# New prices in the build-time planner of a transformer layer, and pair sums in twos for two head groups of each unit

## The chip, the cores and the metric

One core of a Trainium2 chip runs the whole kernel. The metric is the device time in microseconds (us). The engines are TensorE (PE; its weight loads are a row of their own, PEld), VectorE (DVE), ScalarE (ACT), GpSimd (POOL) and SyncE (SP), whose queue issues the DMAs. Each engine works through its own list of instructions strictly in order; semaphores hold an instruction until what it needs is done.

## What is computed

A pre-norm transformer layer on 2048 tokens of width 1024, with 32 heads of 32, and an FFN of width 3584, in bf16:

```
h  = x + softmax(q k^T / sqrt(32)) v @ wo,   q, k, v = layernorm(x) @ wqkv
h2 = h + gelu(layernorm(h) @ w1 + b1) @ w2 + b2       # gelu in its tanh form
```

## The kernel before

**Units, jobs, rounds.** The tokens are cut into 8 units of 256 queries, the heads into 8 groups of 4. A job is one unit with one group (64 jobs), a round is 256 keys of a job (8 rounds). In a round PE makes the scores of four heads as 8 small matmuls in row tiles (`qk`, L787), ScalarE takes the exp in two instructions of 128 x 1024 (L797, 1024 in all), and PE multiplies by V in column tiles (`pv`, L840). Scores go through three pairs of PSUM banks; a new `qk` needs two pairs.

**Denominators.** VectorE adds the two key blocks of a round into a tile PS (L855, "pair sum"), and PE multiplies PS by a matrix of ones, 4 matmuls (`den`, L878). Where `QUAD(qb, g)` is true, VectorE also adds the pair sums of two rounds (L861), and one `den` step serves both. The last round of a job goes to PE without any sum, and so do all rounds of the first two jobs. `QUAD` is `qb < QA or g < QG`, with QA = 2 and QG = 0: true for units 0 and 1. `finish` transposes the denominators (L895), copies the numerators (L902), inverts (L906), transposes back (L907) and multiplies (L909).

**The rest ("background").** Layer norm: `bn_stats` twice and `bn_aggr` on VectorE, a power on POOL, a `tensor_scalar`; then transposes on PE and their eviction (L613, L620 on ScalarE, L622 on VectorE). Projections go through `mm`, with full tiles (L541, L544) or as four narrow ones (L538). For every unit follow wo (eviction L949), a layer norm, ffn1 (14 blocks, eviction with the bias into gT on VectorE, L1018), gelu and ffn2 (output L1070). All of this uses two PSUM banks, 6 and 7, shared with the jobs' accumulators. Gelu works on 1024 columns: x*x (L1038), an affine step (L1039), times x (L1040), all on VectorE, each reading the one before; tanh on ScalarE (L1041, 49 times); plus one (L1042) and times x (L1043) on VectorE. The last unit's gelu is one instruction on ScalarE.

**The order.** Nothing is ordered by hand. `Graph.schedule` plays the whole program through at build time: each task has a price `occ` (how long it holds its engine) and a latency `lat` (how long after that a reader can start), and whenever an engine is free it takes a ready task by priority and then by number. Pair sums have priority -2, the reads of `finish` and the evacuations by ScalarE and the tanh -1, evictions 0, gelu's VectorE steps 1; on PE `qk` goes first, `pv` and `den` come in batches, background fills. SP's DMAs are tasks of the same play. The resulting lists are what the engines get. Prices set the order alone: `assign` puts semaphore waits on all dependences; for engines other than PE this includes a dependence on an earlier instruction of the same engine:

```
elif d.eng != t.eng or t.eng != E.PE:      # kept as a wait
```

`release` sets when a task counts as ready. It leaves out the latency for a dependence within PE, whose instructions follow one another without a wait.

Of the kernel before, what the change touches and what calls it, by code (L numbers as in the profile page):

```python
# [8 lines left out]
ALU = mybir.AluOpType  # L9
AX = mybir.AxisListType  # L10
E = mybir.EngineType

P = 128
# [47 lines left out]
class Graph:  # L61
# [47 lines left out]
    def schedule(self, pick_pe, pool, switch=0.1, dma_rate=280.0, dma_lat=2.1, dma_issue=0.06):  # L109
# [11 lines left out]
        n = 0  # L121
        num = {t: i for i, t in enumerate(self.tasks)}

        def release(t):
            t.ready = max([d.done - (d.lat if d.eng == t.eng == E.PE else 0.0) for d in t.deps], default=0.0)
            heapq.heappush(upcoming[t.eng], (t.ready, num[t], t))
            heapq.heappush(events, t.ready)

# [5 lines left out]
        def free_banks(now):  # L134
            out = []
            for b, u in pool.items():
                if isinstance(u, list) and all(x.done is not None and x.done <= now + 1e-9 for x in u):
                    out.append(b)
            return out

        while n < total:
# [5 lines left out]
            for e in self.ENGS:  # L147
                while free[e] <= now + 1e-9:
# [31 lines left out]
                    if e == E.SP:  # L180
                        k = min(range(self.n_lanes), key=lambda i: lanes[i].done if lanes[i] else 0.0)
# [147 lines left out]
def build_kernel(nc, A_x, A_wqkv, A_wo, B_w1, B_b1, B_w2, B_b2, out):  # L329
    _, S, D = A_x.shape  # L330
# [9 lines left out]
    EPS_BF = 1.0013580322265625e-05  # L340
# [11 lines left out]
    gr = Graph(N_LANES)  # L352
# [65 lines left out]
    rr, B_rr = sb(top, "rr", [P, 2, 8], F32, 2)  # L418
# [51 lines left out]
    psum = nc.alloc_psum_tensor("ps", [P, 8, 512], F32)  # L470
# [11 lines left out]

    MM = 0.2195
    def c_dve_ps(n):
        return (120 + n) / 960.0 + 0.02

    def c_dve(n, x=1):
        return (62 + n / x) / 960.0 + 0.02

    def c_tt(n):  # L490
        return n / 1920.0 + 0.155

    def c_ts(n):
        return n / 3840.0 + 0.165

    GELU_PRIO = 1

    def c_act(n, ap_bias=False):
        return 0.073 + (0.093 if ap_bias else 0.0) + n / 1200.0

    def pe(fns, occ, reads=(), writes=(), kind="bg", mode="full", prio=0, after=()):
        return gr.add(E.PE, fns, occ, 0.16, reads, writes, prio, kind, mode, after)
# [13 lines left out]
    def bi(bank):  # L516
        return bank.n if isinstance(bank, Slot) else bank

    def bb(bank):
        return bank.buf if isinstance(bank, Slot) else B_ps[bank]  # L520
# [26 lines left out]
        return t  # L547

    def act(fn, n, reads=(), writes=(), prio=0, ap_bias=False, kind="", after=()):
        return gr.add(E.Activation, fn, c_act(n, ap_bias), 0.14, reads, writes, prio, kind, after=after)  # L550

    def dve(fn, occ, reads=(), writes=(), prio=0):
        return gr.add(E.DVE, fn, occ, 0.08, reads, writes, prio)

    def pool(fn, occ, reads=(), writes=(), prio=0):
        return gr.add(E.Pool, fn, occ, 0.1, reads, writes, prio)

    def dma(out_ap, in_ap, nbytes, reads=(), writes=(), prio=0, noncontig=False, after=()):
        def fn(s):
# [10 lines left out]
         reads=[B_ident], writes=[B_ident])  # L570
# [8 lines left out]
    def layer_norm(tiles, prio, norm="dve", quick=False):  # L579

        n = len(tiles)
        while cnt["ln"] % NLN + n > NLN:
            cnt["ln"] += 1
        i = cnt["ln"] % NLN
        cnt["ln"] += n
        for k, (x_ap, B_x, o_ap, B_o) in enumerate(tiles):
            for c in range(2):
                dve(lambda v, c=c, k=k, x_ap=x_ap: v.bn_stats(st_l[:, i + k, 6 * c:6 * c + 6], x_ap[:, 512 * c:512 * c + 512]),  # L588
                    0.68, reads=B_x if isinstance(B_x, list) else [B_x], writes=[B_stl[i + k]], prio=prio)
            dve(lambda v, k=k: v.bn_aggr(mv_l[:, i + k, :], st_l[:, i + k, :]), 0.2,  # L590
                reads=[B_stl[i + k]], writes=[B_mv[i + k]], prio=prio)
        sl = slice(i, i + n)
        if quick:
            dve(lambda v: v.tensor_copy(mvb[:, sl, :], mv_l[:, sl, :]), 0.17, reads=B_mv[sl], writes=B_mvb[sl], prio=prio)
            dve(lambda v: v.tensor_scalar(tb[:, sl, :], mvb[:, sl, 1:2], EPS_BF, None, ALU.add), 0.17,
                reads=B_mvb[sl], writes=B_tb[sl], prio=prio)
        else:
            pool(lambda g: g.tensor_copy(mvb[:, sl, :], mv_l[:, sl, :]), 0.25, reads=B_mv[sl], writes=B_mvb[sl], prio=prio)
            pool(lambda g: g.tensor_scalar(tb[:, sl, :], mvb[:, sl, 1:2], EPS_BF, None, ALU.add), 0.25,
                 reads=B_mvb[sl], writes=B_tb[sl], prio=prio)  # L600
        dve(lambda v: v.tensor_copy(mvr[:, sl, :], mvb[:, sl, 0:1]), 0.17, reads=B_mvb[sl], writes=B_mvr[sl], prio=prio)
        pool(lambda g: g.tensor_tensor(denb[:, sl, 0], tb[:, sl, 0], cexp[:, 0:n], ALU.pow), 0.42 + 0.157 * n,
             reads=B_tb[sl] + [B_cexp], writes=B_denb[sl], prio=prio)
        dve(lambda v: v.reciprocal(rden[:, sl, 0], denb[:, sl, 0]), 0.19, reads=B_denb[sl], writes=B_rden[sl], prio=prio)
        for k, (x_ap, B_x, o_ap, B_o) in enumerate(tiles):
            eng, cost = (dve, 0.58) if norm == "dve" else (pool, 3.8)
            eng(lambda e, k=k, x_ap=x_ap, o_ap=o_ap: e.tensor_scalar(
                o_ap, x_ap, mvr[:, i + k, :], rden[:, i + k, :], ALU.subtract, ALU.mult), cost,
                reads=(B_x if isinstance(B_x, list) else [B_x]) + [B_mvr[i + k], B_rden[i + k]], writes=[B_o], prio=prio)

    def transposes(src_ap, B_src, bank, dst_ap, B_dst, evac, prio):
        for dc in range(DC):
            t = pe(lambda p, dc=dc: p.transpose(psb[:, bi(bank), dc * P:(dc + 1) * P], src_ap[:, dc * P:(dc + 1) * P], ident[:]),  # L613
                   0.064, reads=[B_src, B_ident], writes=[bb(bank)], prio=prio)
            take(t, bank)

        def src():
            return psb[:, bi(bank), :].rearrange("p (dc t) -> p dc t", dc=DC)
        if evac == "act":
            t = act(lambda a: a.activation(dst_ap, src(), ACT.Copy), 1024, reads=[bb(bank)], writes=[B_dst], prio=-1)  # L620
        else:
            t = dve(lambda v: v.tensor_copy(dst_ap, src()), 0.70, reads=[bb(bank)], writes=[B_dst])  # L622
        drop(t, bank)


# [178 lines left out]

    closing = set()
    QA = 2
    QG = 0
    DA = 0

    def QUAD(qb, g):  # L810
        return qb < QA or g < QG

# [3 lines left out]
    class Job:  # L816
# [69 lines left out]
        def finish(self):  # L886
            qb, g, bank, nq = self.qb, self.g, self.bank, self.nq
            u = qb % 3
            o = cnt["od"] % 2
            cnt["od"] += 1  # L890
            B_O, B_D = B_OD[o]
            final = self.final
            od, dd = OD[:, o, 0, 0:nq], OD[:, o, 1, 0:nq]
            D = dd.rearrange("p (b j) -> p b j", j=32)
            t = dve(lambda v: v.transpose(dd, psum[:, bi(bank), nq:2 * nq]), c_dve_ps(nq),  # L895
                    reads=[self.B_O, self.B_D], writes=B_D, prio=-1)
            drop(t, bank)
            if final:
                t = act(lambda a: a.activation(od, psum[:, bi(bank), 0:nq], ACT.Copy), nq,
                        reads=[self.B_O, self.B_D], writes=B_O, prio=-1, after=[t])  # L900
            else:
                t = dve(lambda v: v.tensor_copy(od, psum[:, bi(bank), 0:nq]), c_dve_ps(nq),  # L902
                        reads=[self.B_O, self.B_D], writes=B_O, prio=-1)
            drop(t, bank)
            nb = nq // 32
            dve(lambda v: v.reciprocal(rr[:, o, 0:nb], D[:, :, 0]), 0.15, reads=B_D, writes=[B_rr[o]], prio=0)  # L906
            dve(lambda v: v.transpose(D, rr[:, o, 0:nb].unsqueeze(2).to_broadcast([P, nb, 32])), c_dve(nq),  # L907
                reads=[B_rr[o]], writes=B_D, prio=0)
            dve(lambda v: v.tensor_tensor(OT[:, u, g, 0:nq], od, dd, ALU.mult), c_dve(nq),  # L909
                reads=B_O + B_D, writes=B_OT[u][g][0:nq // P], prio=1)  # L910
# [437 lines left out]
```

## Time and profile before

| | |
|---|---|
| runs | 1092.40, 1092.58, 1096.39 us; median 1092.58 |
| profiled execution | 1093.21 us, span 1091.4 us |
| PE busy | 1047.8 us (96%) |
| ScalarE busy | 1019.5 us (93%) |
| VectorE busy | 789.4 us (72%) |
| POOL busy | 28.2 us (3%) |
| DMA | 175.44 MB, mean 161 GB/s |
| exp L797 | 1024 of 128 x 1024, mean 1168 ns, 954.0 us busy |
| pair sum L855 | 432, mean 687 ns, 288.5 us busy |
| sum of two pair sums L861 | 42, mean 687 ns, 28.9 us busy |
| den L878 from PS | 1560 matmuls of 128 x 32 by 256 |

The duration of an instruction is not the time from its start to the next one's: on VectorE and ScalarE instructions overlap in part, on PE they are pipelined and their ends are modelled, so a busy PE is not a PE at its peak. The first exp starts at 16.2 us and the last at 1027.3 us.

### The profile page before, as it was taken

To read this page: it belongs to the slowest core of one execution; us is meant where nothing else is said; L and a number is where in the kernel's file an instruction comes from. 1 tells how busy PE (TensorE), PEld (TensorE's weight loads), DVE (VectorE), ACT (ScalarE), POOL (GpSimd) and SP (SyncE) were. 2 spreads that over 40 slices of the span, in tenths; PEclk is the share of its full clock that TensorE was granted. 3 is DMA by queue.
4 is the path that set the end of the run, shared out by engine and by line. 5 is a ranking of instruction groups with operands and counts; after the bars stand their busy time and mean duration, and the time that the engine had idled before them with its cause. 6 is when DMAs were issued, how large, how long until landed. Compare 5 with 4: busy or idle time off the path is not lost.

```text
span 1091.4 us, 41529 instructions
## 1 busy us (share of the span) xinstructions
PE 1047.8 (96%) x18880; PEld 610.0 (56%) x18930; DVE 789.4 (72%) x1518; ACT 1019.5 (93%) x1124; POOL 28.2 (3%) x78
## 2 busy tenths in 40 slices
PE   7999999998999999999999999999999999999998
PEld 5655555553457446644565466447545754664483
DVE  7657777777778958886589669857885877786511
ACT  4889999999999999999999999999999999999750
POOL 2100000000000000000000000000000000000000
PEclk9999999999899999999999999999999999999999
DMA  7920120035366547555665486467566655975740
GB/s 190 250 83 2 41 83 5 2 133 181 118 186 181 165 154 238 166 174 183 219 176 158 151 249 183 139 193 224 147 199 201 182 173 153 330 225 178 236 156 20
DMA packets 266224, 175.44 MB, mean 161 GB/s; under 512 B 26944, under 2 KB 260416, under 8 KB 265664
## 3 DMA queue, kind: packets, MB, share of 16 engines
q1 hardware_dynamic: 266048, 172.79, 52.0%
q8 instruction: 148, 2.42, 0.9%
q14 instruction: 28, 0.23, 0.1%
HBM read 162.27 MB, written 10.49 MB: 158 GB/s over the span
## 4 chain that ended last, share of the span: by engine, by line
ACT 75%; PE 23%; DVE 1%; issue 1%; DMA 0%; SPq 0%
ACT PT L797 71%; PE ps L541 6%; PE ps L544 5%; PE ps L538 5%; ACT tg L1041 3%; PE ps L787 3%; PE ps L840 2%; PE ps L878 1%; ACT xnT L620 1%; DMA xrb<-in_A_x_dram 0%; PE ps L613 0%; SPq L563 0%; DVE gT L1018 0%; DVE xnT L622 0%; DVE st L588 0%
## 5 line engine op out<-in xcount | busy, mean ns | idle before, releaser
L797 ACT ACTIVATE PT<-ps 128x1024 bf16<-128x1024 f32 x1024 | 954.0, 1168 | 15.9 <-PE ps L787 15.8
L855 DVE TENSOR_TENSOR PS<-PT 128x1024 bf16<-128x1024 bf16 x432 | 288.5, 687 | 121.5 <-ACT PT L797 60.4
L787 PE MATMUL ps<-QT,KT 32*128 32x256 bf16 x4096 | 204.2, 273 | 11.6 <-ACT PT L797 8.1
L840 PE MATMUL ps<-PT,V 128*32 128x256 bf16 x4096 | 176.9, 273 | 2.1 <-ACT PT L797 1.3
L787 PEld LDWEIGHTS ps<-QT,KT 32*128 32x128 bf16 x4096 | 60.9, 92 | 174.0 <-ACT PT L797 162.4
L840 PEld LDWEIGHTS ps<-PT,V 128*32 128x32 bf16 x4096 | 105.0, 97 | 30.8 <-issue 8.3
L541 PE MATMUL ps<-hnT,a_w1r 128*128 128x256 bf16 x906 | 111.5, 273 | 0.7 <-DVE rr L906 0.3
L541 PE MATMUL ps<-a_w2r,gT 128*128 128x512 bf16 x430 | 106.6, 380 | 4.4 <-issue 1.6
L878 PE MATMUL ps<-PS,ones 128*32 128x256 bf16 x1560 | 109.7, 274 | 1.1 <-DVE PS L855 0.5
L538 PE MATMUL ps<-hnT,a_w1r 128*32 128x256 bf16 x2648 | 96.2, 274 | 7.3 <-DVE gT L1018 2.4
L541 PEld LDWEIGHTS ps<-hnT,a_w1r 128*128 128x128 bf16 x906 | 82.8, 98 | 24.8 <-issue 14.5
L538 PE MATMUL ps<-a_w2r,gT 128*32 128x512 bf16 x1304 | 96.5, 381 | 0.1
L1018 DVE TENSOR_TENSOR gT<-ps,b1f 128x512 bf16<-128x512 f32 x98 | 67.3, 687 | 25.5 <-PE ps L538 15.7
L538 PEld LDWEIGHTS ps<-hnT,a_w1r 128*32 128x32 bf16 x2648 | 65.3, 96 | 24.2 <-issue 18.1
L541 PEld LDWEIGHTS ps<-a_w2r,gT 128*128 128x128 bf16 x458 | 39.7, 98 | 52.6 <-issue 12.6
L1041 ACT ACTIVATE tg<-tg 128x1024 bf16<-128x1024 bf16 x49 | 57.9, 1185 | 0.0
L541 PE MATMUL ps<-xnT,Wall 128*128 128x512 bf16 (+1 forms) x238 | 52.2, 354 | 3.4 <-issue 1.3
L878 PEld LDWEIGHTS ps<-PS,ones 128*32 128x32 bf16 x1560 | 41.9, 96 | 17.5 <-issue 5.7
L541 PE MATMUL ps<-a_w1r,OT 128*128 128x512 bf16 x191 | 49.4, 393 | 0.0
L538 PEld LDWEIGHTS ps<-a_w2r,gT 128*32 128x32 bf16 x1304 | 29.2, 96 | 23.1 <-issue 15.0
L895 DVE STREAM_TRANSPOSE OD<-ps 128x256 f32<-128x256 f32 x64 | 28.6, 446 | 12.8 <-PE ps L878 6.5
L1070 DVE SCALAR_TENSOR_TENSOR b_ost<-ps,hch 128x512 bf16<-128x512 f32 x4 | 2.8, 692 | 45.3 <-PE ps L544 45.3
(92 smaller groups left out, 995.1 us busy)
## 6 DMA issues: line engine op xcount, KB each, us to landing
a_w2r<-in_B_w_dram SPq DMA_DIRECT2D x105, 512.0 KB, 5.5
a_w1r<-in_B_w_dram SPq DMA_DIRECT2D x98, 512.0 KB, 4.4
a_w1r<-in_A_wo_dram SPq DMA_DIRECT2D x32, 512.0 KB, 4.2
b_w1r<-in_B_w_dram SPq DMA_DIRECT2D x14, 512.0 KB, 5.3
a_w1r<-in_A_wqkv_dram SPq DMA_DIRECT2D x11, 512.0 KB, 4.5
xrb<-in_A_x_dram SPq DMA_DIRECT2D x16, 256.0 KB, 4.3
Wall<-in_A_wqkv_dram SPq DMA_DIRECT2D x16, 256.0 KB, 4.3
a_w2r<-x_scratch SPq DMA_DIRECT2D x8, 512.0 KB, 4.5
```

The lines of the kernel that those rows point to most:

```text
L538: fns.append(lambda p, j=j: p.matmul(psum[32 * j:32 * j + 32, bi(bank), c0:c1], lhsT[:, 32 * j:32 * j + 32], rhs, start=start, stop=stop, ...
L541: t.whole = lambda p: p.matmul(psum[:, bi(bank), c0:c1], lhsT, rhs, start=start, stop=stop, skip_group_check=True)
L544: t = pe(lambda p: p.matmul(psum[:, bi(bank), c0:c1], lhsT, rhs, start=start, stop=stop), occ, reads=reads, writes=[bb(bank)], mode="full" ...
L620: t = act(lambda a: a.activation(dst_ap, src(), ACT.Copy), 1024, reads=[bb(bank)], writes=[B_dst], prio=-1)
L787: return p.matmul(psum[:, 2 * us[h // 2] + h % 2, n * i:n * i + n], KT[32 * h:32 * h + 32, g, k0:k0 + P], QT[32 * h:32 * h + 32, qs, 0:n], ...
L797: act(lambda a, u=u, k=k: a.activation(PT[:, s, k, :, :], psum[:, 2 * u:2 * u + 2, :], ACT.Exp, bias=0.0, scale=SCALE), 1024, reads=[B_ps[ ...
L840: fns.append(lambda p, i=i, h=h: p.matmul(psum[32 * h:32 * h + 32, bi(bank), 0:nq], V[:, g, nk * r + i, 32 * h:32 * h + 32], PT[:, s, h // ...
L855: dve(lambda v: v.tensor_tensor(PS[:, n, :, :], pairs[:, :, 0:256], pairs[:, :, 256:512], ALU.add), c_dve(1024, 2), reads=[B_PT[2 * s], B_ ...
L878: fns.append(lambda p, h=h, rhs=rhs, i=i: p.matmul(psum[32 * h:32 * h + 32, bi(bank), nq:2 * nq], ones32[:, :], rhs, start=False, stop=las ...
L895: t = dve(lambda v: v.transpose(dd, psum[:, bi(bank), nq:2 * nq]), c_dve_ps(nq), reads=[self.B_O, self.B_D], writes=B_D, prio=-1)
L1018: drop(dve(lambda v: v.tensor_tensor(gT[:, fc:fc + 2, cs], psum[:, bi(bank), 0:2 * n].rearrange("p (f c) -> p f c", f=2), b1f[:, fc:fc + 2 ...
L1041: act(lambda a: a.activation(t, t, ACT.Tanh, bias=0.0, scale=math.sqrt(2.0 / math.pi)), c, reads=B_t, writes=B_t, prio=-1)
```

## The change

Three things, in one diff.

1. **Prices.** On VectorE and ScalarE, `occ` was close to an instruction's duration; it becomes the interval from one start to the next. An addition of 1024 columns goes from 0.688 to 0.600 us in gelu (and from 0.618 to 0.600 as a pair sum), an affine step of 1024 from 0.432 to 0.332, an eviction of 512 fp32 columns from 0.678 to 0.600, a `bn_stats` from 0.68 to 0.60, an exp or tanh of 1024 from 0.926 to 0.915. Latencies grow: ScalarE from 0.14 to 0.165, VectorE from 0.08 to 0.135.
2. **The release rule.** The latency is left out for a dependence within any engine, no longer within PE alone. The waits that are emitted stay as they are.
3. **QG = 2.** `QUAD` is true for head groups 0 and 1 of every unit.

```
-            t.ready = max([d.done - (d.lat if d.eng == t.eng == E.PE else 0.0) for d in t.deps], default=0.0)
+            t.ready = max([d.done - (d.lat if d.eng == t.eng else 0.0) for d in t.deps], default=0.0)
...
     def c_dve_ps(n):
-        return (120 + n) / 960.0 + 0.02
+        return n / 960.0 + 0.067
     def c_dve(n, x=1):
-        return (62 + n / x) / 960.0 + 0.02
+        return n / x / 960.0 + 0.067
     def c_tt(n):
-        return n / 1920.0 + 0.155
+        return n / 1920.0 + 0.067
     def c_ts(n):
-        return n / 3840.0 + 0.165
+        return n / 3840.0 + 0.065
...
     def c_act(n, ap_bias=False):
-        return 0.073 + (0.093 if ap_bias else 0.0) + n / 1200.0
+        return 0.0615 + (0.093 if ap_bias else 0.0) + n / 1200.0
...
-        return gr.add(E.Activation, fn, c_act(n, ap_bias), 0.14, reads, writes, prio, kind, after=after)
+        return gr.add(E.Activation, fn, c_act(n, ap_bias), 0.165, reads, writes, prio, kind, after=after)
...
-        return gr.add(E.DVE, fn, occ, 0.08, reads, writes, prio)
+        return gr.add(E.DVE, fn, occ, 0.135, reads, writes, prio)
...
-                    0.68, reads=B_x if isinstance(B_x, list) else [B_x], writes=[B_stl[i + k]], prio=prio)
-            dve(lambda v, k=k: v.bn_aggr(mv_l[:, i + k, :], st_l[:, i + k, :]), 0.2,
+                    0.6, reads=B_x if isinstance(B_x, list) else [B_x], writes=[B_stl[i + k]], prio=prio)
+            dve(lambda v, k=k: v.bn_aggr(mv_l[:, i + k, :], st_l[:, i + k, :]), 0.117,
...
-            eng, cost = (dve, 0.58) if norm == "dve" else (pool, 3.8)
+            eng, cost = (dve, 0.46) if norm == "dve" else (pool, 3.8)
...
-            t = dve(lambda v: v.tensor_copy(dst_ap, src()), 0.70, reads=[bb(bank)], writes=[B_dst])
+            t = dve(lambda v: v.tensor_copy(dst_ap, src()), 0.59, reads=[bb(bank)], writes=[B_dst])
...
     QA = 2
-    QG = 0
+    QG = 2
...
-            t = dve(lambda v: v.transpose(dd, psum[:, bi(bank), nq:2 * nq]), c_dve_ps(nq),
+            t = dve(lambda v: v.transpose(dd, psum[:, bi(bank), nq:2 * nq]), 0.366,
...
-            dve(lambda v: v.reciprocal(rr[:, o, 0:nb], D[:, :, 0]), 0.15, reads=B_D, writes=[B_rr[o]], prio=0)
-            dve(lambda v: v.transpose(D, rr[:, o, 0:nb].unsqueeze(2).to_broadcast([P, nb, 32])), c_dve(nq),
+            dve(lambda v: v.reciprocal(rr[:, o, 0:nb], D[:, :, 0]), 0.105, reads=B_D, writes=[B_rr[o]], prio=0)
+            dve(lambda v: v.transpose(D, rr[:, o, 0:nb].unsqueeze(2).to_broadcast([P, nb, 32])), 0.366,
```

The small steps of the layer norm (copies, the addition of epsilon, the reciprocal) go from 0.17 and 0.19 to 0.07 to 0.08 in the same way.

More of the change, by code (lines that the diff above doesn't have):

```diff
@@ L593, in layer_norm @@
         if quick:
-            dve(lambda v: v.tensor_copy(mvb[:, sl, :], mv_l[:, sl, :]), 0.17, reads=B_mv[sl], writes=B_mvb[sl], prio=prio)
-            dve(lambda v: v.tensor_scalar(tb[:, sl, :], mvb[:, sl, 1:2], EPS_BF, None, ALU.add), 0.17,
+            dve(lambda v: v.tensor_copy(mvb[:, sl, :], mv_l[:, sl, :]), 0.08, reads=B_mv[sl], writes=B_mvb[sl], prio=prio)
+            dve(lambda v: v.tensor_scalar(tb[:, sl, :], mvb[:, sl, 1:2], EPS_BF, None, ALU.add), 0.08,
                 reads=B_mvb[sl], writes=B_tb[sl], prio=prio)
@@ L600, in layer_norm @@
                  reads=B_mvb[sl], writes=B_tb[sl], prio=prio)
-        dve(lambda v: v.tensor_copy(mvr[:, sl, :], mvb[:, sl, 0:1]), 0.17, reads=B_mvb[sl], writes=B_mvr[sl], prio=prio)
+        dve(lambda v: v.tensor_copy(mvr[:, sl, :], mvb[:, sl, 0:1]), 0.07, reads=B_mvb[sl], writes=B_mvr[sl], prio=prio)
         pool(lambda g: g.tensor_tensor(denb[:, sl, 0], tb[:, sl, 0], cexp[:, 0:n], ALU.pow), 0.42 + 0.157 * n,
              reads=B_tb[sl] + [B_cexp], writes=B_denb[sl], prio=prio)
-        dve(lambda v: v.reciprocal(rden[:, sl, 0], denb[:, sl, 0]), 0.19, reads=B_denb[sl], writes=B_rden[sl], prio=prio)
+        dve(lambda v: v.reciprocal(rden[:, sl, 0], denb[:, sl, 0]), 0.075, reads=B_denb[sl], writes=B_rden[sl], prio=prio)
         for k, (x_ap, B_x, o_ap, B_o) in enumerate(tiles):
-            eng, cost = (dve, 0.58) if norm == "dve" else (pool, 3.8)
+            eng, cost = (dve, 0.46) if norm == "dve" else (pool, 3.8)
             eng(lambda e, k=k, x_ap=x_ap, o_ap=o_ap: e.tensor_scalar(
```

## The prediction

> **What bounds the kernel now.** I read the page's busy shares first, then the busy time by stretches, the chain of waits, and last the timeline where two instructions meet.
>
> ```profile
> PE 1047.8 (96%) x18880; PEld 610.0 (56%) x18930; DVE 789.4 (72%) x1518; ACT 1019.5 (93%) x1124; POOL 28.2 (3%) x78
> ACT 75%; PE 23%; DVE 1%; issue 1%; DMA 0%; SPq 0%
> ```
>
> Two engines look full, and ScalarE carries three quarters of the chain. The shares are averages over three different stages, so here are the stages (columns: length, then busy PE, PEld, DVE, ACT, POOL with counts, granted clock, DMA share, GB/s):
>
> ```profile
> 0.00:66.00 66.00, 56.62 (x979) 38.50 (x983) 44.14 (x110) 44.20 (x48) 11.07 (x34) 1.00 0.77 216
> 66.00:1028.50 962.50, 931.82 (x17461) 533.03 (x17495) 733.24 (x1381) 956.50 (x1041) 15.61 (x42) 1.00 0.52 160
> 1028.50:1091.40 62.90, 59.40 (x454) 38.45 (x456) 11.98 (x28) 18.84 (x36) 1.54 (x2) 1.00 0.36 121
> ```
>
> The head (66 us) ends when the exps become continuous; the tail (62.9 us, PE busy 59.4) is the last unit's FFN behind the last exp. Between them ScalarE is idle for 962.5 - 956.5 = 6.0 us. That is the first limit on any reordering: no order makes the 992 exps and 49 tanhs there shorter.
>
> ```profile
> 67.61 206.38 ACT PT L797 x225
> 274.66 3.10 PE ps L541 x7
> 278.30 1.89 PE ps L541 x6
> ```
>
> In the chain, 225 exps follow one another at 206.38 / 225 = 0.917 us. The old price of one is 0.073 + 1024/1200 = 0.926 us, the new one 0.915: the new one is right, and the old plan gave every round of two exps 0.023 us too much. Going over the starts on ScalarE from 66 to 1028.5 us, I find 11 places where an exp starts over 0.2 us later than the shortest interval allows, 8.9 us in sum: 1.8 + 0.4 at 278 and 281, 1.6 at 415, and 0.2 to 1.2 at 258, 336, 451, 684, 729, 743, 947 and 986. This is what a better order can win in the middle.
>
> The first of these is not the order's. PE's clock is halved there:
>
> ```profile
> 266.00:270.00 4.00, 2.27 (x52) 0.68 (x40) 2.53 (x4) 4.00 (x5) 0.00 (x0) 1.00 0.89 265
> 270.00:274.00 4.00, 1.68 (x36) 0.67 (x36) 2.13 (x7) 4.00 (x6) 0.00 (x0) 0.80 0.57 196
> 274.00:278.00 4.00, 3.96 (x23) 1.16 (x23) 2.29 (x4) 2.73 (x3) 0.00 (x0) 0.50 0.07 20
> ```
>
> PE has run out of background work before unit 0's last group is finished, is busy for 2.27 and then 1.68 of 4 us, and gets clock 0.50 when wo's matmuls at last come; the exps then wait 2.2 us.
>
> Next, what VectorE's new prices say against what it does:
>
> ```profile
> 989.36 0.68 DVE L1043 TENSOR_TENSOR gT<-tg,gT 128x1024 bf16<-128x1024 bf16 x1
> 989.97 0.69 DVE L1040 TENSOR_TENSOR tg<-tg,gT 128x1024 bf16<-128x1024 bf16 x1
> 990.57 0.68 DVE L1038 TENSOR_TENSOR tg<-gT 128x1024 bf16<-128x1024 bf16 x1
> 991.29 0.43 DVE L1039 TENSOR_SCALAR tg<-tg 128x1024 bf16<-128x1024 bf16 x1
> 991.75 0.69 DVE L1040 TENSOR_TENSOR tg<-tg,gT 128x1024 bf16<-128x1024 bf16 x1
> ```
>
> Independent additions start 0.60 to 0.61 us apart although each lasts 0.69; that is the new price (1024/1920 + 0.067 = 0.600). But L1039 reads what L1038 wrote, and starts 0.72 after it, and L1040 starts 0.46 after L1039, where the new price is 0.332. A dependent instruction waits on VectorE's own semaphore, and the new release rule leaves this out: 0.12 us too little at each dependence. The old plan had it slightly too long (0.688 + 0.08 = 0.768).
>
> **The change part by part.** The profiled execution took 1093.21 us, 1.8 more than its span, and 0.6 more than the median of the runs (1092.58). The sum is made against 1093.2, and 0.6 comes off at the end.
>
> *Denominator matmuls.* QG = 2 reaches units 2 to 7 (0 and 1 have their sums in twos already), two head groups each: 12 jobs. Of seven summed rounds of a job, six pair up: 3 denominator steps fewer per job, 36 in all, 144 matmuls.
>
> ```profile
> 992.72 0.28 PE L878 MATMUL ps<-PS,ones 128*32 128x256 bf16 x4
> 992.83 0.39 PE L840 MATMUL ps<-PT,V 128*32 128x256 bf16 x8
> ```
>
> A step holds PE until the next one starts, 0.11 us: 36 x 0.11 = 3.9 us of PE. By time, these jobs lie at 66 to 80, 288 to 303, 397 to 429, 523 to 554, 647 to 681, 776 to 808 and 903 to 932 us. In five of the seven the chain is ScalarE alone, and PE's time is hidden. In two (397, 647) PE's lines hold some 40% of it: there 2 windows x 6 steps x 0.11 x 0.4 = 0.5 us comes off. Bounds 0 and -3.9; I take -0.5, as only one of the 11 late exps lies in these windows.
>
> *Added sums.* 36 VectorE additions, each behind the addition that it reads: 0.60 us hidden behind another, 0.72 by L1038 to L1039: 21.6 to 25.9 us.
>
> ```profile
> 397.00:429.00 32.00, 30.02 (x600) 17.80 (x597) 18.97 (x36) 30.76 (x34) 0.00 (x0) 1.00 0.68 211
> 647.00:681.00 34.00, 33.18 (x697) 24.06 (x693) 30.68 (x58) 34.00 (x38) 0.00 (x0) 1.00 0.63 179
> ```
>
> In the first window VectorE idles for 13.0 us, which covers 6 x 0.72 = 4.3. In the second it idles for 3.3, and 1.0 sticks out. The additions have priority -2, so evictions of PSUM banks (0) and the gelu steps (1) queue behind them, and PE's next background group waits for the eviction. Bounds 0 and +4.3 (the whole of that window's six); I take +0.5.
>
> *ScalarE's price.* Each round is planned 0.023 us shorter, so less background work stands ahead of each qk. The rounds from 319 to 326 us are paced by PE at 1.86 us where ScalarE needs 1.83: this is the excess that goes. Of the 8.9 us I leave the clock's 2.2 (the projections still end before unit 0 does) and the 1.6 at 415, where PE waited 1.5 us before a qk while ScalarE stood idle, so for something else, most likely the query tile's DMA. Of the other 5.1, bounds are 0 and -5.1; I take -3.0, since several of the waits (743, 947, 986) are single stops of PE of 0.4 to 0.7 us with "issue" as their cause, which an order shortens but does not remove. The background work put off is no loss until the tail, where 30 ffn2 matmuls now fill the wait for the last layer norm.
>
> *The release rule.* A gelu is three dependent steps, then a tanh on ScalarE, whose place in ScalarE's queue is fixed; every exp behind it waits if it is late. Two dependences x 0.12 = 0.24 us too early in the plan. How much margin is there? From the end of L1040 to the start of its tanh I find 0.03 to 1.43 us over the 49, median 0.53, seven under 0.24; now no tanh waits. If the margins stay spread like one ScalarE interval (0 to 0.92), the mean loss is 0.24 x 0.24 / 2 / 0.92 = 0.031 us, 49 x 0.031 = +1.5 us. Bounds 0 and 49 x 0.24 = +11.8.
>
> [...]
>
> *Layer norms and the ends.* Equal readiness now goes by number, so two bn_stats of a tile, today mostly interleaved with another tile's, stand in a row: 16 tiles x 3 x 0.12 = 5.8 us more on VectorE in the head, which idles there for 66 - 44.1 = 21.9 us. Some will be on the path, and a changed interleaving of evacuations and exps can win as well. Bounds -3 and +5.8, taken 0. Smaller prices (transposes, reciprocal, evictions) shift places only: 0.
>
> Sum: -0.5 + 0.5 - 3.0 + 1.5 = -1.5, so 1093.2 - 1.5 - 0.6 = 1091.1, say 1091.0.
>
> **The rivals.** *Late tanhs* (slower): in stretches where VectorE is nearly full (30.7 of 34 us) lateness adds up, and most tanhs are late by the full 0.24 us: +11.8 at most; with two thirds of it, and the other terms as above less 1.5, 1091.0 + 7.9 - 1.5 = 1097.4, and with the evictions late in the same way (98 of them, a third x 0.12 = 3.9) 1101. It decides once more than half of the margins are under 0.24 us. For it: the 0.12 in every dependent pair. Against it: the median margin of 0.53, and VectorE's 24% idle in the middle.
>
> *The waits go* (faster): the tighter ScalarE price and the relieved PE remove nearly all of 8.9 us: 1092.6 - 8.9 = 1083.7. For it: PE-paced stretches are just where the old price was loose. Against: clock, DMA and issue stops are in no price.
>
> *The change does little*: the orders differ, but ScalarE's floor of 956.5 us in the middle stays, the 36 steps were hidden; 1092.6. It lies within my forecast's range.
>
> **How the numbers follow.** About 0.5% (5.5 us) is what a measurement of this kernel tells from no change: 1087.1 to 1098.0. Forecast, with the do-little case: 0.51, its own range 1087.1 to 1098.0. The waits go: 0.25, reaching to 1083.7, and to 1082 with 2 us won in the head. Late tanhs: 0.24, to 1101. The range 1082 to 1101 leaves out the far ends of head and tanh bounds.
>
> **What would show it.** Right: ScalarE in the middle still at 0.917 us an exp; L861 at 78 instead of 42, the L878 steps from PS at 1416 matmuls instead of 1560; chain mostly L797; late exps adding up to 5 to 8 us. Wrong on the slow side: ScalarE's L1041 with idle time before it, released by DVE L1040, or PE waits on DVE gT of over 10 us. Wrong on the fast side: ScalarE's idle in the middle under 2 us with the clock never halved, or a head clearly under 66 us. If the tail grows past 65 us, put-off background work was not free.

## The result, and the profile after

The kernel became slower by 0.4%: median 1097.84 us (1097.42 to 1099.81) against 1094.22 us for the kernel before run beside it (1092.58 in its earlier runs), ratio 1.0040 [1.0028, 1.0053]. That lies within the 0.5% that were called no change, but the interval is clear of 1, and on the other side than the forecast of 1091.0. The profiled execution took 1099.26 us, its span is 1097.5.

The kernel after, busy shares, the chain by engine and by line, and three groups of instructions (count, then busy time and mean ns of one, then the idle time before them and what ended it):

```profile
PE 1049.3 (96%) x19041; PEld 605.6 (55%) x19092; DVE 808.9 (74%) x1554; ACT 1021.2 (93%) x1124; POOL 29.5 (3%) x78
ACT 52%; PE 28%; DVE 16%; issue 2%; DMA 1%; POOL 0%; SPq 0%; POOLq 0%; DVEq 0%
...
ACT PT L797 50%; PE ps L541 8%; PE ps L538 6%; PE ps L544 5%; PE ps L787 4%; DVE PS L855 3%; PE ps L840 3%; ACT tg L1041 3%; DVE st L588 2%; DVE gT L1018 2%; PE ps L878 1%; DVE PS L861 1%; DVE tg L1040 1%; DMA q_scratch<-lq 1%; DVE tg L1038 1%
...
L878 PE MATMUL ps<-PS,ones 128*32 128x256 bf16 x1416 | 99.4, 274 | 4.8 <-issue 2.4
...
L1041 ACT ACTIVATE tg<-tg 128x1024 bf16<-128x1024 bf16 x49 | 55.7, 1137 | 0.9 <-DVE tg L1040 0.6
L861 DVE TENSOR_TENSOR PS<-PS 128x1024 bf16<-128x1024 bf16 x78 | 54.0, 692 | 2.7
```

The change does what it says: 78 sums of two pair sums, 1416 matmuls from PS. The busy shares hardly moved. What moved is the chain: ScalarE's share fell from 75% to 52%, VectorE's rose from 1% to 16%. Such a share says where the chain runs, not how much time is lost there (an example stands under ScalarE's price below).

By stretches (columns as before). The cuts are the starts of the 33rd and of the last exp, the same in every kernel below; they give 65.7, 961.6 and 64.1 us for the kernel before. Here the kernel after:

```profile
0.00:66.50 66.50, 56.90 (x936) 38.13 (x940) 44.63 (x110) 43.65 (x47) 10.82 (x34) 1.00 0.76 214
66.50:1032.50 966.00, 932.66 (x17651) 529.09 (x17700) 752.76 (x1418) 957.26 (x1040) 17.18 (x42) 1.00 0.52 159
1032.50:1097.50 65.00, 59.71 (x470) 38.36 (x463) 11.48 (x27) 20.32 (x38) 1.54 (x2) 1.00 0.35 120
```

The middle is 966.0 - 961.6 = 4.4 us longer, with ScalarE's busy time about the same (957.3). ScalarE's starts tell where. In these traces the shortest usual interval from one start to the next is 0.904 us behind an exp and 0.945 behind a tanh. At these, the middle's 1040 intervals would take 991 x 0.904 + 49 x 0.945 = 942.2 us; what a middle has beyond that is lateness, before an exp or before a tanh. In sum the exps start 19.0 us late in the kernel before and 20.6 after, the tanhs 0.5 and 3.2. So some 1.6 of the 4.4 us stand before exps and 2.7 before tanhs. Of starts over 0.2 us late there are 25 with 14.7 us in sum (19 exps and 6 tanhs), where there were 11 with 8.9, all exps. Head and tail add 0.8 and 0.9 us.

A stretch of the middle, the kernel after: first the chain (start, length, what; VectorE is idle for 0.6 us in all from 660 to 686 us), then the timeline.

```profile
666.48 0.35 DVE tg L1042
666.85 0.69 DVE gT L1043
667.54 0.35 DVE tg L1039
...
667.92 0.69 DVE tg L1040
668.61 0.68 DVE gT L1018
...
669.42 1.27 PE ps L538 x38
```

```profile
666.85 0.69 DVE L1043 TENSOR_TENSOR gT<-tg,gT 128x1024 bf16<-128x1024 bf16 x1
...
667.46 0.42 DVE L1039 TENSOR_SCALAR tg<-tg 128x1024 bf16<-128x1024 bf16 x1
...
667.92 0.69 DVE L1040 TENSOR_TENSOR tg<-tg,gT 128x1024 bf16<-128x1024 bf16 x1
...
668.58 0.69 DVE L1018 TENSOR_TENSOR gT<-ps,b1f 128x512 bf16<-128x512 f32 x1
...
669.42 1.85 PE L538 MATMUL ps<-hnT,a_w1r 128*32 128x256 bf16 x48 [0.68 <-DVE gT L1018]
...
671.20 0.40 PE L787 MATMUL ps<-QT,KT 32*128 32x256 bf16 x8
```

L1040 stands right behind L1039, whose result it reads, and starts 0.46 us after it where the plan has 0.33, 0.13 us late by this step alone. The eviction L1018 queues behind it and holds the PSUM bank; PE is idle for 0.68 us, and the background group that then starts late puts the next qk to 671.20 and its exp 0.23 us late. In the kernel after, L1039 follows directly on its own L1038 22 times (before: 6), and L1040 on its L1039 25 times (before: 10).

### The profile page after: what moved, and what is told of

The parts are those of the page before. It is cut to its first block, busy times and chain, and to the rows that moved or that the text cites. A ratio compares the mean times of both kernels' runs of the same rounds, so it can differ in the third digit from the quotient of the medians.

```text
span 1097.5 us, 41883 instructions
## 1 busy us (share of the span) xinstructions
PE 1049.3 (96%) x19041; PEld 605.6 (55%) x19092; DVE 808.9 (74%) x1554; ACT 1021.2 (93%) x1124; POOL 29.5 (3%) x78
## 4 chain that ended last, share of the span: by engine, by line
ACT 52%; PE 28%; DVE 16%; issue 2%; DMA 1%; POOL 0%; SPq 0%; POOLq 0%; DVEq 0%
ACT PT L797 50%; PE ps L541 8%; PE ps L538 6%; PE ps L544 5%; PE ps L787 4%; DVE PS L855 3%; PE ps L840 3%; ACT tg L1041 3%; DVE st L588 2%; DVE gT L1018 2%; PE ps L878 1%; DVE PS L861 1%; DVE tg L1040 1%; DMA q_scratch<-lq 1%; DVE tg L1038 1%
## 5 line engine op out<-in xcount | busy, mean ns | idle before, releaser
L538 PE MATMUL ps<-hnT,a_w1r 128*32 128x256 bf16 x2856 | 102.8, 274 | 4.5 <-DVE gT L1018 2.1
L541 PE MATMUL ps<-hnT,a_w1r 128*128 128x256 bf16 x854 | 104.7, 273 | 2.0 <-DVE gT L1018 0.8
L878 PE MATMUL ps<-PS,ones 128*32 128x256 bf16 x1416 | 99.4, 274 | 4.8 <-issue 2.4
L541 PE MATMUL ps<-a_w2r,gT 128*128 128x512 bf16 x400 | 99.9, 380 | 4.0 <-issue 1.4
L538 PE MATMUL ps<-a_w2r,gT 128*32 128x512 bf16 x1420 | 103.0, 381 | 0.0
L541 PEld LDWEIGHTS ps<-hnT,a_w1r 128*128 128x128 bf16 x854 | 78.3, 98 | 24.1 <-issue 13.4
L538 PEld LDWEIGHTS ps<-hnT,a_w1r 128*32 128x32 bf16 x2856 | 70.8, 96 | 23.4 <-issue 18.1
L1018 DVE TENSOR_TENSOR gT<-ps,b1f 128x512 bf16<-128x512 f32 x98 | 67.1, 685 | 14.7 <-PE ps L538 11.3
L1041 ACT ACTIVATE tg<-tg 128x1024 bf16<-128x1024 bf16 x49 | 55.7, 1137 | 0.9 <-DVE tg L1040 0.6
L861 DVE TENSOR_TENSOR PS<-PS 128x1024 bf16<-128x1024 bf16 x78 | 54.0, 692 | 2.7
L541 PE MATMUL ps<-a_w1r,OT 128*128 128x512 bf16 x171 | 43.4, 391 | 0.5 <-DVE lq L712 0.2
L1070 DVE SCALAR_TENSOR_TENSOR a_ost<-ps,hch 128x512 bf16<-128x512 f32 x28 | 19.2, 684 | 24.5 <-PE ps L538 14.1
```

The lines of the kernel that those rows point to most:

```text
L538: fns.append(lambda p, j=j: p.matmul(psum[32 * j:32 * j + 32, bi(bank), c0:c1], lhsT[:, 32 * j:32 * j + 32], rhs, start=start, stop=stop, ...
L541: t.whole = lambda p: p.matmul(psum[:, bi(bank), c0:c1], lhsT, rhs, start=start, stop=stop, skip_group_check=True)
L861: dve(lambda v: v.tensor_tensor(PS[:, n, :, :], PS[:, n, :, :], PS[:, m, :, :], ALU.add), c_dve(1024, 2), reads=[B_PS[n], B_PS[m]], writes ...
L878: fns.append(lambda p, h=h, rhs=rhs, i=i: p.matmul(psum[32 * h:32 * h + 32, bi(bank), nq:2 * nq], ones32[:, :], rhs, start=False, stop=las ...
L1018: drop(dve(lambda v: v.tensor_tensor(gT[:, fc:fc + 2, cs], psum[:, bi(bank), 0:2 * n].rearrange("p (f c) -> p f c", f=2), b1f[:, fc:fc + 2 ...
L1041: act(lambda a: a.activation(t, t, ACT.Tanh, bias=0.0, scale=math.sqrt(2.0 / math.pi)), c, reads=B_t, writes=B_t, prio=-1)
```

## The experiments

In the table, a ratio is to the kernel before, run beside it; the three parts are those of the cuts above; "before exps" and "before tanhs" are by how much the middle's exps and tanhs start later, in sum, than the shortest intervals allow, so that a middle is 942.2 us and these two. (The profile's idle time is less, 0.9 us in the kernel after, because an instruction of ScalarE may start while the one ahead of it still ends.)

| kernel | ratio [95%] | head, middle, tail us | before exps us | before tanhs us | VectorE in the chain |
|---|---|---|---|---|---|
| before | 1 | 65.7, 961.6, 64.1 | 19.0 | 0.5 | 1% |
| after | 1.0040 [1.0028, 1.0053] | 66.5, 966.0, 65.0 | 20.6 | 3.2 | 16% |
| old_release | 1.0002 [0.9991, 1.0012] | 65.4, 963.7, 63.4 | 20.4 | 1.1 | 2% |
| qg0 | 1.0073 [1.0059, 1.0086] | 65.9, 961.9, 68.7 | 16.0 | 3.7 | 9% |
| prices_only | 1.0056 [1.0044, 1.0069] | 65.7, 964.3, 68.0 | 21.8 | 0.4 | 2% |
| release_only | 1.0007 [0.9997, 1.0018] | 64.4, 961.4, 66.1 | 18.5 | 0.7 | 3% |
| qg2_only | 1.0064 [1.0050, 1.0078] | 66.1, 964.3, 68.3 | 21.7 | 0.4 | 2% |
| act_price_only | 1.0108 [1.0093, 1.0122] | 66.7, 961.5, 76.1 | 19.1 | 0.3 | 1% |
| dep_price | 1.0021 [1.0006, 1.0037] | 65.5, 962.3, 65.5 | 19.3 | 0.7 | 8% |
| tanh_later | 1.0127 [1.0111, 1.0144] | 66.7, 968.7, 70.5 | 25.7 | 0.8 | 15% |
| tanh_later_028 | 1.0069 [1.0055, 1.0083] | 66.5, 969.8, 64.8 | 27.3 | 0.3 | 14% |
| tanh_later_045 | 1.0059 [1.0040, 1.0078] | 66.6, 969.8, 63.9 | 27.4 | 0.2 | 13% |
| after_0617 | 1.0058 [1.0040, 1.0076] | 66.8, 967.5, 64.9 | 22.6 | 2.8 | 16% |
| prices_0640 | 0.9997 [0.9982, 1.0012] | 66.3, 965.8, 63.3 | 22.8 | 0.8 | 3% |
| old_release_0670 | 1.0013 [1.0001, 1.0026] | 66.0, 963.3, 63.3 | 20.3 | 0.8 | 3% |
| old_release_0730 | 1.0055 [1.0037, 1.0072] | 66.4, 968.9, 63.6 | 25.1 | 1.6 | 4% |
| rule_gelu | 1.0067 [1.0044, 1.0090] | 64.5, 971.5, 64.3 | 26.8 | 2.6 | 12% |
| rule_rest | 1.0026 [1.0015, 1.0037] | 66.2, 962.4, 68.0 | 19.6 | 0.6 | 7% |
| before_warm | 1.0019 [1.0005, 1.0033] | 67.3, 963.1, 64.3 | 20.7 | 0.2 | 1% |
| old_release_warm | 0.9996 [0.9982, 1.0010] | 65.7, 959.5, 64.9 | 16.9 | 0.5 | 3% |

### The three parts, undone or done alone

**old_release**: the kernel after with the old release rule.

```
-            t.ready = max([d.done - (d.lat if d.eng == t.eng else 0.0) for d in t.deps], default=0.0)
+            t.ready = max([d.done - (d.lat if d.eng == t.eng == E.PE else 0.0) for d in t.deps], default=0.0)
```

> The changed kernel with the old release rule (latency left out within PE alone). Dependence theory (the plan starts a dependent VectorE step 0.12 us too early, so tanhs and evictions come late): ratio to before 0.998 to 1.001, and far fewer than 22 of 49 tanhs at the least margin of 0.03 us. Slack theory (intervals as prices take away what absorbed unplanned stops): still 1.003 to 1.005. Sums theory (the 36 added VectorE additions delay what queues behind them): still 1.003 to 1.005.

Measured 1.0002: the rule costs 0.0040 - 0.0002 = 0.38%, some 4 us, given the other two parts. Its chain by engine:

```profile
ACT 74%; PE 22%; DVE 2%; issue 1%; DMA 0%; SPq 0%; POOL 0%; DVEq 0%
```

VectorE is off the chain again. In the two profiles, undoing the rule takes 1.1 us from the head, 2.3 from the middle and 1.6 from the tail; of the middle's 2.3 us, 2.1 stood before tanhs and 0.2 before exps.

**qg0**: the kernel after with `QG = 0` (new prices, new rule).

> The changed kernel with QG = 0: prices and release rule new, sums in twos as before. Sums theory: ratio to before 0.999 to 1.001. Dependence theory: 1.002 to 1.005, tanhs still late in 15 or more of 49 cases. Slack theory: 1.003 to 1.006, since PE then has 3.9 us more to do as well.

**prices_only**: the kernel after with the old rule and `QG = 0`.

> The kernel before with the new prices and latencies alone, old release rule, QG = 0. Slack theory: 1.003 to 1.005. Dependence theory: 0.997 to 1.001 (a dependent addition is then planned at 0.600 + 0.135 = 0.735, measured 0.72). Sums theory: 0.997 to 1.001.

**release_only**: the kernel before with the new rule.

> The kernel before with the new release rule alone. Dependence theory: 1.002 to 1.004, with tanhs at the least margin in 10 or more cases. Slack theory: 0.999 to 1.001, since the long old prices cover the 0.12 us (0.688 against 0.72 measured). Sums theory: 0.999 to 1.001.

**qg2_only**: the kernel before with `QG = 2`.

> The kernel before with QG = 2 alone. Put-off theory (with the tighter ScalarE price background work moves behind the last exp, and the 3.9 us of denominators pay for it): here nothing was put off beyond what the last layer norm covers, so 0.998 to 1.001 with a tail of 63 to 64 us. If the additions are a gain by themselves (the 0.5% between prices with and without them): 0.994 to 0.997.

None of the three theories fits these runs. The dependence theory has old_release right, but not release_only (1.0007, where it says 1.002 at least) or prices_only (1.0056, where it says 1.001 at most); the slack theory has the other three within their intervals, but not old_release; the sums theory fits release_only alone. qg2_only, at 1.0064, is outside both of its expectations.

Read together, the parts don't add. With the old prices the rule costs 0.07% (not told from nothing); with the new ones 0.17% without the sums in twos (1.0073 against 1.0056; their intervals overlap) and 0.38% with them. Without them the rule doesn't lengthen the middle: qg0's is 2.4 us shorter than prices_only's, although its tanhs start 3.7 us late and those of prices_only 0.4. With the new prices, QG = 2 wins 0.54% under the old rule and 0.33% under the new one; with the old prices it costs 0.64%. Nearly all that QG = 2 does is in the tail: 68.0 to 63.4 and 68.7 to 65.0 us with the new prices, 64.1 to 68.3 with the old. Full ffn2 matmuls of unit 6 left behind the last exp go with it: 47 to 27 and 45 to 26 with the new prices (30 in the kernel before).

The path prices, then QG, then rule reads +0.56%, -0.54%, +0.38%.

### ScalarE's price and the tail

**act_price_only**: the kernel before, with an exp planned at 0.915 instead of 0.926 us.

```
-        return 0.073 + (0.093 if ap_bias else 0.0) + n / 1200.0
+        return 0.0615 + (0.093 if ap_bias else 0.0) + n / 1200.0
```

> The kernel before with ScalarE's price alone changed (0.926 to 0.915 us for an exp). Put-off theory: over 3 us more ffn2 behind the last exp, tail 67 to 68.5 us, 1.003 to 1.005. If VectorE's prices are what costs in the run with all prices: 0.999 to 1.001, tail 64 us.

Measured 1.0108, with a middle no shorter than before (961.5) and a tail of 76.1 us, 12 us longer where the put-off theory had expected 3 to 4. The timeline of PE behind the last exp shows what lies in it:

```profile
1031.02 1.67 PE L541 MATMUL ps<-a_w2r,gT 128*128 128x512 bf16 x7
...
1033.39 4.70 PE L541 MATMUL ps<-a_w2r,gT 128*128 128x512 bf16 x21
...
1041.90 11.60 PE L541 MATMUL ps<-a_w2r,gT 128*128 128x512 bf16 x53
1053.34 6.87 PE L544 MATMUL ps<-hnT,b_w1r 128*128 128x128 bf16 x99
```

With 4 more between these rows, 85 of unit 6's ffn2 matmuls are left behind the last exp, 85 x 0.219 = 18.6 us. The wait for the last layer norm hides some 6 us of that, as it did before; the other 12 are added to the end.

**prices_0640**: prices_only with the exp at 0.917 us (`return 0.064 + …`).

> The run with the new prices alone (old rule, QG = 0), with an exp priced 2.5 ns longer: 0.917 us, what the chip takes, for 0.915. Put-off theory: each round is planned 5 ns longer, 512 rounds give 2.6 us more room for background work ahead of the last exp: tail down from 68.0 to 63.5 to 65.5 us, ratio 1.0056 down to 1.000 to 1.003. If put-off work is not what makes the tail long: 1.005 to 1.006 and 68 us again.

Measured 0.9997. 2.5 ns more on the price of one exp take the tail from 68.0 to 63.3 us; the middle is 1.5 us longer in its profile, with PE's clock halved twice for 3.4 us, which prices_only's profile doesn't show. This is the answer to act_price_only from the other side: the tail follows from how much background the plan leaves to the end, and ns in a price decide that.

**old_release_0670** and **old_release_0730**: old_release with the exp at 0.920 and 0.926 us (the price before).

> As the run before, with an exp at 0.920 us, between the two prices. Put-off theory: tail 63 to 64 us, middle 961 to 965, ratio 0.997 to 1.001; it is the candidate for the fastest. If a tight price is a gain by itself: between the old-rule run and the one at 0.926, 1.001 to 1.002.

> The changed kernel with the old release rule and the old price of an exp (0.926 us). Put-off theory: the tail is already covered in the run with the old rule (63.4 us) and cannot get shorter, 63 to 64; the middle, paced by ScalarE, stays at 961 to 965 us: 0.998 to 1.002. If a tight price of ScalarE is a gain by itself, as the prediction had it (-3 us): 1.002 to 1.004, with a middle of over 966 us.

Measured 1.0013 and 1.0055, the second above both of its expectations. With tails equal within 0.3 us, the middle is 968.9 us at 0.926, 963.3 at 0.920 and 963.7 at 0.915 (with 13.7, 10.2 and 3.4 us of halved clock in the three profiles). So beside the other new prices a tighter price of the exp does win in the middle, 5 us, and all of it by 0.920. In the chain of old_release_0730, PE has the place that ScalarE has in old_release's:

```profile
PE 67%; ACT 25%; DVE 4%; issue 2%; DMA 1%; SPq 0%; POOL 0%; POOLq 0%; DVEq 0%
```

### What of the release rule costs the time

**after_0617**: the kernel after with 0.2 ns more on the exp, to see how far a cost hangs on one order (PE's instructions differ from 120.9 us on).

> The changed kernel with an exp priced 0.2 ns longer (0.0617 for 0.0615 in the formula): nothing that any theory cares for, but the plan's ties fall differently and the lists change from some 190 instructions of TensorE on. It gives the scatter that belongs to the order alone. If the release rule's loss is systematic: 1.002 to 1.006 of before, waits before tanhs over 2 us in the middle, TensorE's waits on VectorE over 14 us. If the loss was this one order's accident: 1.000 or less is as likely as 1.004, with these two waits nearer to the old rule's (1 and 7 us).

Measured 1.0058, slower still, with the same 16% of VectorE in the chain. So the kernel after is no single unlucky order: two orders with the rule are at 1.0040 and 1.0058, and three with the old rule, at a price from 0.915 to 0.920, at 0.9996 (with the added matmuls below), 1.0002 and 1.0013. The 0.18% between the first two isn't told from nothing, as their intervals overlap.

**tanh_later, tanh_later_028, tanh_later_045**: the kernel after, with 0.24, 0.28 and 0.45 us added to the latency of the third gelu step, so that the plan knows when a tanh can start.

```
+                g3.lat += 0.24
```

> The changed kernel, with 0.24 us more latency on the third gelu step, so that tanhs are planned later; nothing else. If late tanhs are what the release rule costs: 1.000 to 1.002, and the waits before tanhs fall from 3.2 to under 1 us in the middle. If PE's waits on VectorE (evictions and sums late, 21 us after, 7 with the old rule) are the larger part: 1.002 to 1.004, with these waits still over 15 us.

> The changed kernel with 0.28 us more latency on the third gelu step (the tanh is planned later by that), release rule new; the plan ends as before (65.3 us behind the last exp). If late tanhs carry the loss in the middle: middle 962.5 to 964.5 us, waits before tanhs under 1, tail 63.5 to 65, head still 66.5: 1.000 to 1.002. If they do not: middle 965.5 to 968, 1.003 to 1.006.

> The same with 0.45 us (plan 64.4 us behind the last exp): a second order for the same question. Late tanhs: middle 962.5 to 964.5, waits before tanhs under 0.8, 1.000 to 1.002. Otherwise: middle 965.5 to 968, 1.003 to 1.006.

The waits before tanhs went from 3.2 us to 0.8, 0.3 and 0.2, and the middle didn't shorten: 968.7, 969.8 and 969.8 us (tanh_later has a longer tail as well, so the other two were chosen with the planned tail of the kernel after). Of the ratios only that of tanh_later_045 lies in a range that was expected. The exps took the place of the tanhs: they start 25.7 to 27.4 us late in sum, where the kernel after has 20.6. A later tanh in the plan re-makes the order behind it, so these runs don't say what the tanhs' waits cost in the kernel after; they say that this edit wins nothing. VectorE keeps its place in the chain, here tanh_later_028:

```profile
ACT 47%; PE 34%; DVE 14%; issue 2%; DMA 2%; POOL 1%; SPq 0%; POOLq 0%; DVEq 0%
```

**dep_price**: the kernel after, where a dependent step of VectorE is planned 0.12 us behind the interval of an independent one, 0.72 us for an addition, as the trace of before has it.

```
-            t.ready = max([d.done - (d.lat if d.eng == t.eng else 0.0) for d in t.deps], default=0.0)
+            t.ready = max([d.done - (d.lat if d.eng == t.eng == E.PE else d.lat - 0.12 if d.eng == t.eng == E.DVE else d.lat if d.eng == t.eng else 0.0) for d in t.deps], default=0.0)
```

> The changed kernel with the release rule mended: for a dependence within VectorE the reader is ready at the end of the price plus 0.015 us less than before's rule would give, that is 0.12 us after it less the latency of 0.135, so a dependent addition is planned 0.615 us behind the one that it reads. If the rule's error of 0.12 us is what costs, part of it stays (0.615 against 0.72 measured): 1.001 to 1.004, PE's waits on VectorE between 7 and 21 us. If only the order by number counts (dependents taken at once), the reader now comes after other ready work and the whole loss goes: 0.999 to 1.001.

(The 0.615 us named there is a slip: the plan has 0.600 + 0.135 - 0.015 = 0.72.) Measured 1.0021, between the kernel after and old_release; its interval touches both, so by its time alone it decides nothing. In its profile VectorE is 8% of the chain and the middle is 3.7 us shorter than after's.

**rule_gelu** and **rule_rest**: the new rule on VectorE only for the tasks of priority 1 (gelu, the second layer norm, the last step of `finish`), and only for the others.

```
rule_gelu:  d.lat if d.eng == t.eng and (d.eng != E.DVE or t.prio == 1) else 0.0
rule_rest:  d.lat if d.eng == t.eng and not (d.eng == E.DVE and t.prio == 1) else 0.0
```

> The changed kernel, with the new release rule on VectorE only for readers of priority 1: the gelu steps, the second layer norm and the last step of finish. If gelu's chain carries the loss in the middle: 1.002 to 1.005, middle 965 to 968 us, waits before tanhs over 2 us, head 65 to 66. If the rest carries it: 0.999 to 1.001, middle under 964.5, waits before tanhs near 1.

> The changed kernel, with the new release rule on VectorE for all other readers: the first layer norm, the first steps of finish, the sums of pair sums. The plan ends with some 4 us more behind the last exp here, so the time is read by parts. If gelu's chain carries the loss: middle 962 to 964.5 us, waits before tanhs near 1 us, TensorE's waits on VectorE near 7. If the rest carries it: middle 965 to 968 and waits over 14. The head is 66.5 us in both cases (65.4 with the old rule).

Measured 1.0067 and 1.0026. The middle is long with the rule on gelu's steps (971.5 us, of which two more halvings of the clock than after has take a part) and short with it on the rest (962.4, with a tail 4.6 us above old_release's). That points to the gelu steps. But PE's idle time that VectorE ended, the other sign named, points to the rest: 19.7 us in rule_rest and 11.2 in rule_gelu, against 21.0 in the kernel after, 7.0 in old_release and 13.2 in the kernel before. Nor do the two add up to the kernel after, so the split among the dependences stays open. (The rule also holds within ScalarE and POOL; no run tries that alone.)

```profile
ACT 62%; PE 29%; DVE 7%; issue 1%; DMA 1%; POOL 0%; SPq 0%; POOLq 0%; DVEq 0%
```

This chain is rule_rest's. Across all kernels, VectorE has 7 to 16% of the chain with the new rule on the new prices, and 1 to 4% otherwise. This share goes with the rule, not with the time: qg0, rule_rest and dep_price, at 9, 7 and 8%, have middles within 1 us of the kernel before.

### The halved clock

**before_warm** and **old_release_warm**: the kernel before, and old_release, with 24 and 18 matmuls added that nobody reads, where PE runs out of work ahead of unit 0's wo.

```
+            t = pe(lambda p, wb=wb: p.matmul(psum[:, bi(wb), 0:512], ident[:, :], b2t[:, 0:512], start=True, stop=True), 0.2225, ...)
```

> The kernel before, with 24 matmuls that nobody reads, which TensorE takes where it has nothing else behind the last projections (planned at 267 to 300 us); the plan's length is the same. If the halved clock costs about 4 us: 0.996 to 0.998, clock 1.0 in most runs. By the prediction's 2.2 us: 0.998. If the exps late there have another cause: 1.000 and more, or a clock still halved.

> The run with new prices, QG = 2 and the old rule, with 18 such matmuls (planned at 267 to 324 us, the plan 1.2 us longer). If the halved clock costs 4 us and comes in most of its runs: 0.996 to 0.998 of before, the fastest of all. If it is rarer there than in the kernel before (3 of 11 runs had none): 0.998 to 1.000.

The mean granted clock was 1.0 in 10 of 12 runs of before_warm and in 8 of 12 of old_release_warm, where the kernel before has 0.994 to 0.998 in most. Yet before_warm came to 1.0019, and its runs at clock 1.0 had a median of 1095.6 us, no less than the kernel before. In its profile no exp from 260 to 334 us is over 0.2 us late, so the 2.2 us after unit 0 are gone; but exps are 2.2 and 1.5 us late at 745 and 748 us, where the kernel before has 0.8 at 743 and the clock is now halved for 3.4 us. old_release_warm, at 0.9996 and a profiled span of 1090.2 us, isn't told from old_release. The added matmuls change all the order behind them, by more than the 2.2 us that the halving was put at, so what it costs stays open.

No kernel here beats the kernel before by more than its interval; the best are old_release_warm, prices_0640 and old_release, all level with it.

## Why the prediction was wrong, point by point

**The bound: right.** ScalarE's busy time in the middle is a floor that no order moved (955.6 to 958.9 us in all kernels), and no kernel won more than 961.6 - 959.5 = 2.1 us there.

**Two steps failed, ScalarE's price and the release rule.** The sum forecast -1.5 us; a ratio of 1.0040 is +4.4. Undoing the rule splits this. With the old rule and all else new the runs give +0.2 us (old_release), where the terms without the rule add up to -3.0, all of it ScalarE's price. The rule gives the other +4.2, where its term was +1.5. So the first is 3.2 us off and the second 2.7. How the first spreads over the price of ScalarE, the prices of VectorE ("shift places only: 0") and the sums in twos depends on the order in which they are put in.

**ScalarE's price, -3.0: no such excess, and a wrong cover.** The term was to come from rounds that PE paces at 1.86 us. The trace of before doesn't have this excess. From 319 to 326 us the chain does run along PE, but the exps keep to their shortest interval; first two pieces of the chain, then the exps:

```profile
320.64 1.53 PE ps L541 x13
322.50 1.53 PE ps L541 x13
```

```profile
319.03 7.58 ACT L797 ACTIVATE PT<-ps 128x1024 bf16<-128x1024 f32 x8
```

The next exp starts at 326.28, so 8 intervals are 0.906 us each. (The qk there start 1.66, 1.86, 1.85 and 1.79 us apart; two of these agree with 1.86.) In the runs the middle's exps start 19.0 us late in sum before, 19.1 with the price alone and 20.6 after, where 3 us less were forecast. The cover was wrong as well: "The background work put off is no loss until the tail" was true, and the tail was the loss, as the 6 us of cover there were already in use. By itself the price costs 12 us in the tail and wins 0.1 in the middle. Beside the other new prices and the sums in twos the middle does win 5 us against a price of 0.926; why it needs them isn't shown. The check named for this, a tail past 65 us, came out at 65.0 in the kernel after, because QG = 2 paid for it (68.7 without it).

**The release rule, +1.5: too small.** The runs give 0.38%, about 4 us. The 0.12 us at each dependence was read rightly. The term counted tanhs alone and held their margins as the trace of before has them; but the new plan spends the margins that it believes it has. Margins under 0.24 us went from 7 to 25 of the 49, those under 0.05 from 2 to 17. Much of that isn't the rule's doing: old_release, with the old rule, has 23 and 12. Between old_release and the kernel after the tanhs' lateness grows by 2.1 us, which is nearly all of the middle's 2.3, and 2.7 us lie in the head and the tail, about which the term didn't ask. These are single profiles. Whether a late step on VectorE costs time by another way, through pair sums, evictions and a held bank, isn't shown: VectorE's place in the chain and PE's waits for it grow with the rule, but over the kernels they don't go with the time. How the rule costs the rest of its 4 us stays open.

**The late tanhs, the slower rival: near in its number, by luck.** It gave 1097.4 us from 7.9 us of late tanhs, with the -3.0 of ScalarE's price kept; the tanhs are 3.2 us late, and the -3.0 didn't come. Its condition, more than half of the margins under 0.24, is met by 25 of 49; but old_release has 23 and is level with the kernel before, so the condition doesn't decide it. Of the signs on the slow side, idle time before L1041 ended by L1040 came (0.6 us); PE waits on DVE gT of over 10 us didn't: 3.0 us, with 2.4 before. The late eviction at 667 us is one of these few.

**Denominators and sums, -0.5 and +0.5: wrong in kind.** Both terms looked at PE and VectorE where the jobs lie. What the 36 steps less are worth shows up at the end, as background that isn't left to the tail (-4.6 and -3.7 us with the new prices). Under the old prices the same edit costs 0.64%. A term of the sum can't hold such an amount: it depends on the other parts.

**The waits go, the faster rival: no.** The waits over 0.2 us rose from 8.9 to 14.7 us. The halving at the end of unit 0 stayed, as said (columns as above, the kernel after):

```profile
266.00:270.00 4.00, 3.82 (x85) 2.13 (x82) 1.09 (x3) 4.00 (x6) 0.00 (x0) 1.00 0.73 219
270.00:274.00 4.00, 2.18 (x52) 0.96 (x44) 3.03 (x5) 2.93 (x4) 0.00 (x0) 0.91 0.52 149
274.00:278.00 4.00, 2.78 (x28) 0.78 (x21) 3.19 (x8) 4.00 (x6) 0.00 (x0) 0.50 0.93 311
```

**Layer norms and head, 0: not settled.** The two bn_stats of a tile do follow each other now, without another tile's between them, and the head is 0.8 us longer, but heads differ by 1.6 us even between equal orders (below).

**The forecast's form.** A sum of terms from the trace of before assumes that the edits act one by one on an order that stays. Here an edit of 2.5 ns or of 36 steps re-makes the order, the parts are worth half a per cent each with either sign, and nearly cancel. The range held the time; the forecast had its direction wrong.

## What to carry to other kernels

In a planner, a price and a release rule belong together: if prices become start-to-start intervals, a dependent step costs more than its price wherever the wait is still emitted. Here undoing the rule brought the time back to that of the kernel before; putting the 0.12 us back (dep_price) left a time that can't be told from either. To find lost time, sum up how late the starts of the pacing engine are against its shortest intervals: an engine's share of the chain can be large where nothing is late. Read what lies behind the last instruction of the pacing engine. Test the parts in pairs, since alone each may show the other sign, and change a price by a nanosecond or less to learn how much of a difference is only the order.

## What the runs showed of the hardware

**Dependent steps of VectorE.** In the kernel after, too, an independent pair is 0.61 us apart (L1043 at 666.85, L1039 at 667.46) and a dependent one further than its price: 0.46 us for L1039 to L1040, with 0.33 planned. The medians there are 0.60 us for independent additions and 0.72 for L1038 to its L1039.

**Granted clock.** It differs among runs of one kernel. Three runs of the kernel before at a mean granted clock of 1.0 took 1089.5 to 1091.3 us, where the medians are 1093.3 us at 0.997 (55 runs) and 1094.65 us at 0.995 (42 runs). A halving lasts 3.4, 6.8 or 10.2 us in the profiles here, multiples of 3.4; some profiles (qg0, prices_only, dep_price, act_price_only, old_release_warm) have none ahead of their last microsecond.

**The head.** before_warm's matmuls are those of the kernel before up to 68.9 us, and yet its 33rd exp starts 1.6 us later. One wait on a query tile's DMA, issued at 64.97 us instead of 61.80, carries most of it; first the kernel before, then before_warm:

```profile
65.21 0.40 PE L787 MATMUL ps<-QT,KT 32*128 32x256 bf16 x8
```

```profile
66.86 0.40 PE L787 MATMUL ps<-QT,KT 32*128 32x256 bf16 x8 [1.22 <-DMA QT<-q_scratch]
```

So a difference of 1 us between two heads, as between before and after, can be the DMA's alone.
